# adaLN + S4D convolution + ReLU network on one NeuronCore: reordering the last kernel group, the transforms of block 0 and two DMA queues

## The chip, the cores and the metric

The kernel runs on one core of one Trainium2 chip. The metric is the device time of one execution in microseconds (us). The names of the engines in the profile are PE (TensorE matmul), PEld (TensorE weight load), DVE (VectorE), ACT (ScalarE), POOL (GpSimd) and SP (SyncE, which here only issues DMAs).

## The reference, cut to what matters

```python
def _A_ref(u, log_A_real, A_imag, C_real, C_imag, log_dt, D_skip):     # L = 2048, D = 576, N = 128
    dt = exp(log_dt); A = -exp(log_A_real) + 1j * A_imag; C = (C_real + 1j * C_imag) * dt[:, None]
    P = exp((A * dt[:, None])[:, :, None] * arange(L))
    K = 2.0 * einsum("dn,dnl->dl", C, P).real          # the generated convolution kernel
    Kf = rfft(K, 2 * L); Uf = rfft(u.T, 2 * L)
    return irfft(Uf * Kf)[:, :, :L].T + u * D_skip
def _B_ref(x, w1, w2):                                 # w1 576 x 4608, w2 4608 x 576
    return relu(x @ w1) @ w2
mod = (silu(c) @ w_mod)                                # 6 rows of 576: sa, ca, ga, sb, cb, gb
h = layernorm(x) * (1 + ca) + sa
x = x + ga * _A_ref(h, ...)
h = layernorm(x) * (1 + cb) + sb
x = x + gb * _B_ref(h, w1, w2)
```

## The kernel before

The sequence of 2048 is cut into 4 blocks of 512. Each block has a convolution part (`conv(s)`: transforms, spectra, products, inverse, second layernorm) and a part of the network (`ffn`, 36 column tiles of the hidden layer, each a `first` into `hps` and a `second` into `acc`). Matmuls are fp32 in two passes or split into a high and a low part in fp32r. Blocks 1 to 3 have their convolution woven into the network of the block before; block 0 has none before it, so everything up to its first `hps` matmul is a prologue.

The prologue generates the convolution kernel. 576 channels go in 6 groups of 96 (`KGen.first`, loop over `g`), each group in two halves `u` of 48. A group builds two factors on ACT, DVE and POOL: `W2` (32 powers) and `W1` (16 powers, by `doubling`: one, two, four, eight times two powers; the last doubling has the tiles `T0`, `T1` of 128 x 768 and its adds on POOL). The `products` of a half are 96 small matmuls, two passes each, from `W1` and `W2` into a PSUM tile `kps`. `rows(g)` copies `kps` into `ke` (ACT), and after every third group `store` writes `ke` to `kd` in DRAM; `load_kt` reads it back transposed as the tile `kt`, `skip` adds `D_skip` to its first row, and `mm_K` transforms it. `save(g)` stores `W1` to `W1d` for the later blocks.

`conv(0)` is a generator, run in `main`; what it yields as a word runs a piece of another: `"first"`, `"late"`, `"rows"` are the two halves of the last group's products and the end of `first` (`save(5)`, `rows(5)`, `store`), `"mod"` a step of `mod_late`, `"weights"`, `"high"`, `"low"` a step of `ffn` (loads of its first weights, their high parts, their low parts). `early` prepares `h`, the normalised and modulated input: its last step is `skip` on the first `kt` and, per row tile, a multiply by `ca` and an add of `sa`. `mm_U(p)` transforms half `p` of `h`, `mm_K(p)` half `p` of the kernel. `spec_U`, `spec_K` are the butterflies that make `U_0`, `U_1`, `K_0`, `K_1`; `product(p)` multiplies them to `Y`, `back` makes `V`, `inverse` transforms it back, and its result is added to `x` on DVE, between the steps of `product(1)`. `mod_late` makes `sb`, `cb` (in front of the network) and `gb` (behind it): loads of three pieces of `w_mod` (`wm_*`, 1.3 MB each), 50 small matmuls each (`mps_*`), a copy, and two transposes for `sb` and `cb` (`mpt_*`).

The order on an engine is that of a scheduler, except where an operation is recorded through `Kept` or `keep_in_program_order` (the profile then shows the helper's line, L47, L59, L62, L65, L68 or L71): those keep their written order against each other. Spectra tiles (`Z`, `W`, `U`, `K`, `Y`, `V`) share 6 buffers, and a tile starts only when the readers of its buffer, stores to DRAM included, are done. DMAs that an engine issues stand in its instruction queue and wait there in order.

Of the kernel before, what the change touches and what calls it, by code (L numbers as in the profile page):

```python
# [18 lines left out]
P = 128  # L19
# [30 lines left out]
class KGen:  # L50
# [274 lines left out]
    def first(self, setup, mod):  # L325
# [26 lines left out]
        def rows(g):  # L352
            qs = slice(24 * (g % 3), 24 * (g % 3) + 24)
            self.act(ke[:, :, qs], ps[g].rearrange("p q a -> p a q"), AF.Copy)
            if g % 3 == 2:
                self.store(0, g // 3, ke.rearrange("p a q -> p (a q)"), nc.sync)

# [39 lines left out]
        for g in range(NG):  # L397
# [26 lines left out]
            else:  # L424
                run(late, double[3])
            if g + 1 == NG:
                next(early)
            if g > 0:
                rows(g - 1)
            run(*double[4:])  # L430
            if g + 1 < NG:
                save(g)
# [141 lines left out]
class Body:  # L574
# [34 lines left out]
    def early(self, kg):  # L609
# [25 lines left out]
        for i in (0, 2, 1, 3):  # L635
            kept(nc.scalar.activation(
                h[:, i], x2[:, i], AF.Identity, scale=mv[:, i, 3:4], bias=mv[:, i, 4:5]
            ))
        yield
        self.kt0 = kg.kt0  # L640
        kept(self.skip(self.kt0, 0, nc.vector))
        for i in (0, 2, 1, 3):
            kept(nc.vector.tensor_tensor(h[:, i], h[:, i], self.m["ca"], op=ALU.mult))
            kept(nc.vector.tensor_tensor(h[:, i], h[:, i], self.m["sa"], op=ALU.add))
# [93 lines left out]
    def mod_late(self):  # L738


        nc, act, cb = self.nc, self.nc.scalar.activation, self.cb
        for j, nm in ((3, "sb"), (4, "cb"), (5, "gb")):
            self.mod_weights(self.wm[nm], slice(j * D, (j + 1) * D), nc.sync)
        for nm in ("sb", "cb", "gb"):
            yield
            w = self.wm[nm]
            ps = self.cps.tile([P, 512], F32, tag="cps", bufs=self.nps, name=f"mps_{nm}")
            self.mod_products(ps, cb, w, nc.tensor.matmul)
            row = self.cv.tile([P, 2 * P], F32, tag="row", bufs=1, name=f"row_{nm}")
            act(row[:, 0:P], ps[:, 0:P], AF.Copy)  # L750
            for o in (P, P + 64):
                act(row[0:32, o : o + 64], ps[0:32, P : P + 64], AF.Copy)
            if nm == "gb":
                yield
                self.mod_spread(row, self.md[nm], self.m[nm], Kept(self.tc, nc.gpsimd))
                return
            ps = self.cps.tile([P, 512], F32, tag="cps", bufs=self.nps, name=f"mpt_{nm}")
            nc.tensor.transpose(ps[:, 0:P], row[:, 0:P], self.ident)
            nc.tensor.transpose(ps[:, P : P + 32], row[0:32, P:], self.ident[:32, :32])
            act(  # L760
                self.m[nm], ps[:, 0 : 5 * 32].rearrange("p (j r) -> p j r", r=32)[:, :, 0],
                AF.Copy, bias=1.0 if nm == "cb" else 0.0,
            )

# [174 lines left out]
    def conv(self, s):  # L939
# [18 lines left out]
        def kernel_tile(p):  # L958
            t = self.cv.tile([P, 16, 72], F32, tag="kt", bufs=1, name="kt")
            self.load_kt(t, s, p, nc.gpsimd if s else nc.sync)  # L960
            return t

        kt = [kernel_tile(0) if s else self.kt0, None]
        yield -1 if s else "mod"
        if s:
# [15 lines left out]
        def spec_U(p, Z):  # L981
            U = self.spec(f"U_{s}_{p}")
            yield from self.butterfly(Z, U, -1)
            yield -1
            if s + 1 < NB or p == 1:
                self.save(self.Ud[s][p], U)
            Us.append(U if s == 0 or p == 0 else None)
# [87 lines left out]
        if s == 0:  # L1075
            yield from mm_K(0, ZK)
            yield from mm_U(0, ZU)
            Z1 = self.spec("Z")
            yield from mm_U(1, Z1)
            for hook in ("first", "late", "rows"):  # L1080
                yield hook
            kt[1] = kernel_tile(1)
            yield "weights"
            yield "mod"
            yield "mod"
            yield "mod"
            yield "high"
            yield from spec_U(0, ZU)
            yield from spec_U(1, Z1)
            yield from spec_K(0, ZK)  # L1090
            ZK = self.spec("Z")
            yield from mm_K(1, ZK)
            self.save(self.Rd[0][0], Ks[0], Kept(self.tc, nc.gpsimd))
        else:
            yield from both(self.norm1(x2, h), mm_K(0, ZK))
            kt[1] = kernel_tile(1)
            ZU = self.spec("Z")
            yield from both(spec_K(0, ZK), mm_U(0, ZU))
# [166 lines left out]
    def ffn(self, gens):  # L1265
# [166 lines left out]
        yield  # L1432
        lo1(0)
        lo2(0)
        lo1(1)
        yield
        load_r2(1)
# [200 lines left out]
```

## Time and profile before

| | |
|---|---|
| time, median of 3 runs | 1326.89 us |
| lowest, highest | 1318.24, 1328.18 us |
| the profiled execution's own time | 1322.81 us |
| its span (first to last instruction) | 1321.0 us |
| mean granted TensorE clock | 0.946 |
| PE busy over the span | 1210.7 us (92%) |
| DVE busy | 895.0 us (68%) |
| ACT busy, POOL busy | 494.8 us (37%), 160.3 us (12%) |
| PE busy from 345 us to the end | 961.21 of 976.00 us |
| DVE busy from 260 to 345 us | 83.71 of 85.00 us |

Times in the profile count from the span's first instruction. The first network matmul of block 0 (`hps`) starts at 220.30 us. A row of the timeline reads: start, duration, engine, line, operation, output<-inputs, shapes, count, and in brackets the idle time of the engine before it with what ended it.

### The profile page before, as it was taken

Reading aid. Unit: us, or ns where it says so; the run is one execution under the profiler, and the core shown is the slowest. Engines: PE = TensorE matmul, PEld = TensorE weight load, DVE = VectorE, ACT = ScalarE, POOL = GpSimd, SP = SyncE. Lnnn points to the kernel's source line nnn. Section 1 sums busy time; section 2 is a strip of 40 time slices with the busy share of each in tenths; the row PEclk is TensorE's granted clock in tenths of the full one; section 3 lists DMA queues with packets and bytes.
Section 4 is the critical chain, followed back from the end, with each engine's and each line's share of the span. In section 5 each row is a group of like instructions: output and inputs, shape, how many; then the busy total and the mean of one; then the engine's idle time right before and its main releaser. Section 6 shows DMA issues by size and latency. Waiting matters only on the chain.

```text
span 1321.0 us, 25994 instructions
## 1 busy us (share of the span) xinstructions
PE 1210.7 (92%) x10720; PEld 959.5 (73%) x10720; DVE 895.0 (68%) x1324; ACT 494.8 (37%) x863; POOL 160.3 (12%) x256
## 2 busy tenths in 40 slices
PE   4666686999999998999999999999999999999998
PEld 2444564677767776787777887887888888888886
DVE  7889988999976999589468994557996222111112
ACT  5787523222223422622243225433323452233231
POOL 1666411011000100110011000100000000000000
PEclk9556787999899999999999999999999999999999
DMA  8757982988778977799889985868996667666662
GB/s 274 269 200 289 322 304 85 349 308 322 286 256 303 345 241 262 261 406 336 279 276 336 360 323 156 294 198 294 343 382 198 172 179 227 202 194 197 195 178 71
DMA packets 118027, 345.85 MB, mean 262 GB/s; under 512 B 17772, under 2 KB 19604, under 8 KB 107156
## 3 DMA queue, kind: packets, MB, share of 16 engines
q1 hardware_dynamic: 101332, 228.14, 51.9%
q0 software_dynamic: 16064, 114.67, 23.0%
q8 instruction: 84, 1.38, 0.4%
q10 hardware_dynamic: 512, 1.38, 0.4%
q14 instruction: 35, 0.29, 0.1%
HBM read 262.73 MB, written 81.40 MB: 261 GB/s over the span
## 4 chain that ended last, share of the span: by engine, by line
PE 75%; DVE 14%; DMA 6%; issue 4%; ACT 1%; POOL 1%; SPq 0%; ACTq 0%; DVEq 0%; POOLq 0%
PE hps L1332 31%; PE acc L1358 30%; PE ps_f L852 5%; PE kps L519 3%; PE kps L71 2%; DMA L1d<-w 2%; PE ph L71 2%; PE ps_i L1059 2%; DVE T L484 1%; DVE W1r L486 1%; DMA x<-in_x_dram 1%; DVE T L62 1%; DMA Ua<-Ud 1%; DVE W L62 1%; DVE w L1302 1%
## 5 line engine op out<-in xcount | busy, mean ns | idle before, releaser
L1332 PE MATMUL hps<-xh,w 128*128 128x512 f32 x1152 | 394.2, 403 | 0.8 <-ACT xh L47 0.8
L1358 PE MATMUL acc<-w,hh 128*128 128x512 f32 x1136 | 362.1, 401 | 4.9 <-ACT hh L1337 3.4
L1338 DVE SCALAR_TENSOR_TENSOR hl<-hps,hh 128x512 fp32r<-128x512 f32 x144 | 99.2, 689 | 306.9 <-ACT hh L1337 306.2
L1332 PEld LDWEIGHTS hps<-xh,w 128*128 128x128 f32 x1152 | 217.8, 190 | 48.3 <-ACT xh L47 1.4
L1358 PEld LDWEIGHTS acc<-w,hh 128*128 128x128 f32 x1136 | 212.5, 188 | 51.3 <-ACT hh L1337 4.3
L1332 PE MATMUL hps<-xl,w 128*128 128x512 f32 x576 | 227.4, 396 | 0.0
L1358 PE MATMUL acc<-w,hl 128*128 128x512 f32 x568 | 221.0, 402 | 1.6 <-DVE hl L1338 1.6
L1337 ACT ACTIVATE hh<-hps 128x512 fp32r<-128x512 f32 x144 | 86.0, 597 | 324.7 <-PE hps L1332 317.5
L1307 ACT ACTIVATE w<-r 128x576 fp32r<-128x576 f32 x141 | 96.7, 686 | 229.0 <-PE acc L1358 221.4
L1332 PEld LDWEIGHTS hps<-xl,w 128*128 128x128 f32 x576 | 109.1, 189 | 22.9
L1358 PEld LDWEIGHTS acc<-w,hl 128*128 128x128 f32 x568 | 106.9, 190 | 25.3 <-DVE hl L1338 3.0
L1297 ACT ACTIVATE w<-r 128x640 fp32r<-128x640 f32 x140 | 102.6, 733 | 40.6 <-DMA L1d<-w 38.1
L1332 PE MATMUL hps<-xs,w 128*128 128x512 f32 x288 | 98.3, 411 | 0.0
L71 PE MATMUL kps<-W,W 128*32 128x16 f32 x2304 | 40.3, 211 | 44.9 <-POOL W L68 28.4
L1038 DVE TENSOR_TENSOR Y<-Y,T 128x1152 f32<-128x1152 f32 x60 | 79.4, 1351 | 0.0
L71 PEld LDWEIGHTS kps<-W,W 128*32 128x32 f32 x2304 | 35.5, 145 | 58.8 <-POOL W L68 31.0
L853 ACT ACTIVATE Z<-ps_f 128x288 f32<-128x288 f32 x120 | 48.9, 409 | 71.9 <-PE ps_f L852 70.1
L519 PEld LDWEIGHTS kps<-W1r,W2r 128*32 128x32 f32 x3456 | 45.1, 113 | 37.8 <-issue 23.1
L519 PE MATMUL kps<-W1r,W2r 128*32 128x48 f32 (+2 forms) x3456 | 52.5, 201 | 14.4 <-issue 8.8
L1332 PEld LDWEIGHTS hps<-xs,w 128*128 128x128 f32 x288 | 53.5, 189 | 11.2
L1358 PE MATMUL acc<-hh,w 128*128 128x512 f32 x142 | 56.7, 399 | 0.0
L1358 PE MATMUL acc<-hl,w 128*128 128x512 f32 x142 | 56.0, 394 | 0.0
(249 smaller groups left out, 1543.5 us busy)
## 6 DMA issues: line engine op xcount, KB each, us to landing
r<-in_w_dram SPq DMA_DIRECT2D x144, 320.0 KB, 5.9
r<-in_w_dram SPq DMA_DIRECT2D x144, 288.0 KB, 3.6
w<-L1d SPq DMA_DIRECT2D x108, 320.0 KB, 3.9
w<-L2d SPq DMA_DIRECT2D x108, 288.0 KB, 2.7
W2r<-W2d POOLq DMA_DIRECT2D x18, 1536.0 KB, 8.8
W2d<-W SPq DMA_DIRECT2D x12, 1536.0 KB, 8.5
Ua<-Ud POOLq DMA_DIRECT2D x15, 1152.0 KB, 9.4
W<-W1d POOLq DMA_DIRECT2D x18, 768.0 KB, 9.4
```

The costliest lines, as they stand in the source:

```text
L62: self.tc.keep_in_program_order(self.nc.vector.tensor_tensor(out, a, b, op=op))
L71: self.tc.keep_in_program_order(self.nc.tensor.matmul(*args, **kw))
L519: nc.tensor.matmul(ps[32 * dd : 32 * dd + 32, q, :], W2[:, r, ch], W1[:, r, ch], start=(r == 0), stop=(r == 1),)
L852: nc.tensor.matmul(o, fc[:, n2, c, :], src(n2), start=True, stop=True)
L853: ev = nc.scalar.activation(Z[:, n2, c], ps[:, :PC], AF.Copy)
L1038: v(y, y, T, op=op or ALU.add)
L1297: copy(g - 1)(w1[g][:, 0], r1[g], AF.Copy)
L1307: copy(g)(w[:, 0:D], r2[g], AF.Copy)
L1332: nc.tensor.matmul(ps, a, x, start=(i == 0), stop=(i == 13))
L1337: nc.scalar.activation(hh, ps, AF.Relu)
L1338: nc.vector.scalar_tensor_tensor(hl, ps, 0.0, hh, op0=ALU.max, op1=ALU.subtract)
L1358: nc.tensor.matmul(acc[i], a, x, start=(f == 0 and seen[i] == 1), stop=(f == NF - 1 and seen[i] == (3 if i < 4 else 2)),)
```

## The change

- `KGen.first`, last group: the step of `early` that shifts `h` is called behind the last doublings, not ahead of them; the `skip` of the first `kt` moves into the step before.
- `conv(0)`: the transforms and the last group's products alternate: `mm_K(0)`, first half of the products, `mm_U(0)`, second half and `rows`, `mm_U(1)`. The spectrum of `K_0` is made ahead of those of `U_0` and `U_1`.
- SP's queue: `W1d`, `kd` and `kt` of the last group stand ahead of the loads of `wm_sb`, `wm_cb`, `wm_gb`.
- `mod_late`: its matmuls stand behind `mm_K(1)`; the transposes of one piece stand behind the matmuls of the next.
- POOL's queue: the stores `Ud_0`, `Rd_0`, `Ud_1` of block 0's spectra stand in this order behind the `skip` of the second `kt`.
- `ffn`: its first loads (`"weights"`) come behind the spectra's stores; `"high"` and `"low"` come behind `inverse(0)`, and of the three low parts only the first stands there; the second and third come after the second layernorm.

```diff
@@ KGen.first
-                self.store(0, g // 3, ke.rearrange("p a q -> p (a q)"), nc.sync)
+                self.store(0, g // 3, ke.rearrange("p a q -> p (a q)"), Kept(self.tc, nc.sync))
...
                 run(late, double[3])
-            if g + 1 == NG:
-                next(early)
             if g > 0:
                 rows(g - 1)
             run(*double[4:])
+            if g + 1 == NG:
+                next(early)
@@ Body.early
-        yield
         self.kt0 = kg.kt0
         kept(self.skip(self.kt0, 0, nc.vector))
+        yield
         for i in (0, 2, 1, 3):
             kept(nc.vector.tensor_tensor(h[:, i], h[:, i], self.m["ca"], op=ALU.mult))
@@ Body.mod_late
-            self.mod_weights(self.wm[nm], slice(j * D, (j + 1) * D), nc.sync)
+            self.mod_weights(self.wm[nm], slice(j * D, (j + 1) * D), Kept(self.tc, nc.sync))
+        yield
+        rows = {}
         for nm in ("sb", "cb", "gb"):
-            yield
-            w = self.wm[nm]
             ps = self.cps.tile([P, 512], F32, tag="cps", bufs=self.nps, name=f"mps_{nm}")
...
-            row = self.cv.tile([P, 2 * P], F32, tag="row", bufs=1, name=f"row_{nm}")
+            row = rows[nm] = self.cv.tile([P, 2 * P], F32, tag="row", bufs=2, name=f"row_{nm}")
...
+            nm = {"cb": "sb", "gb": "cb"}.get(nm)
+            if nm:
+                row = rows[nm]
+                ps = self.cps.tile([P, 512], F32, tag="cps", bufs=self.nps, name=f"mpt_{nm}")
+                nc.tensor.transpose(ps[:, 0:P], row[:, 0:P], self.ident)
+                nc.tensor.transpose(ps[:, P : P + 32], row[0:32, P:], self.ident[:32, :32])
...
+            yield
+        self.mod_spread(rows["gb"], self.md["gb"], self.m["gb"], Kept(self.tc, nc.gpsimd))
@@ Body.conv
-            self.load_kt(t, s, p, nc.gpsimd if s else nc.sync)
+            self.load_kt(t, s, p, nc.gpsimd if s else Kept(self.tc, nc.sync))
...
-            if s + 1 < NB or p == 1:
+            if s and (s + 1 < NB or p == 1):
                 self.save(self.Ud[s][p], U)
...
             yield from mm_K(0, ZK)
+            yield "first"
             yield from mm_U(0, ZU)
+            yield "late"
+            yield "rows"
             Z1 = self.spec("Z")
             yield from mm_U(1, Z1)
-            for hook in ("first", "late", "rows"):
-                yield hook
             kt[1] = kernel_tile(1)
-            yield "weights"
             yield "mod"
-            yield "mod"
-            yield "mod"
-            yield "high"
+            yield from spec_K(0, ZK)
             yield from spec_U(0, ZU)
             yield from spec_U(1, Z1)
-            yield from spec_K(0, ZK)
             ZK = self.spec("Z")
             yield from mm_K(1, ZK)
-            self.save(self.Rd[0][0], Ks[0], Kept(self.tc, nc.gpsimd))
+            for dst, t in (
+                (self.Ud[0][0], Us[0]), (self.Rd[0][0], Ks[0]), (self.Ud[0][1], Us[1])
+            ):
+                self.save(dst, t, Kept(self.tc, nc.gpsimd))
+            for _ in range(3):
+                yield "mod"
+            yield "weights"
...
         if s == 0:
-            yield "low"
             yield from spec_K(1, ZK)
...
             yield from inv
+            yield "high"
+            yield "low"
             yield "mod"
@@ Body.ffn
         lo1(0)
+        yield
+        lo1(1)
         lo2(0)
-        lo1(1)
-        yield
```

**PE**, from the end of the fifth group's products to the inverse transform. `kps_1942` is the fifth group, `kps_2248` the sixth (its two rows are the two halves), `ps_f<-kt_1943` is `mm_K(0)`, `ps_f<-h_2099` is `mm_U`, `ps_f<-kt` is `mm_K(1)` (16 rows, of which the first stands here). Before:

```order
L71 MATMUL kps_1942<-W_4_1712,W_9_1706 32x16 x96
L852 MATMUL ps_f<-kt_1943,fcK 128x288 x8
L852 MATMUL ps_f<-h_2099,fcU 128x288 x16
L71 MATMUL kps_2248<-W_5_2048,W_10_2041 32x16 x96
L71 MATMUL kps_2248<-W_5_2048,W_11_2042 32x16 x96
L733 MATMUL mps_sb<-wm_sb,cb 32x128 x20
L758 MATMUL mpt_sb<-ident,row_sb 128x128
L733 MATMUL mps_cb<-wm_cb,cb 32x128 x19
L758 MATMUL mpt_cb<-ident,row_cb 128x128
L733 MATMUL mps_gb<-wm_gb,cb 32x128 x19
L891 MATMUL ps_f<-kt,fcK 128x288
L1059 MATMUL ps_i<-V_0_2753,gc 128x288 x6
```

The same place with the change:

```order
L71 MATMUL kps_1942<-W_4_1712,W_9_1706 32x16 x96
L854 MATMUL ps_f<-kt_1943,fcK 128x288 x8
L71 MATMUL kps_2248<-W_5_2048,W_10_2041 32x16 x96
L854 MATMUL ps_f<-h_2099,fcU 128x288 x8
L71 MATMUL kps_2248<-W_5_2048,W_11_2042 32x16 x96
L893 MATMUL ps_f<-kt,fcK 128x288
L733 MATMUL mps_sb<-wm_sb,cb 32x128 x20
L733 MATMUL mps_cb<-wm_cb,cb 32x128 x20
L757 MATMUL mpt_sb<-ident,row_sb 128x128
L733 MATMUL mps_gb<-wm_gb,cb 32x128 x20
L757 MATMUL mpt_cb<-ident,row_cb 128x128
L1062 MATMUL ps_i<-V_0_2746,gc 128x288 x6
```

The sixth group's halves now stand on either side of the first `mm_U` (a second row of 8 `ps_f<-h_2099` follows the second half), and the modulation's matmuls have moved from ahead of `mm_K(1)` to between it and the inverse transform `ps_i`.

**SP**, the DMA queue behind the stores of the last `W2` factors. Before:

```order
L723 DMA wm_sb<-in_w_mod_dram 128x4x576
L723 DMA wm_gb<-in_w_mod_dram 128x4x576
L723 DMA wm_cb<-in_w_mod_dram 128x4x576
L360 DMA W1d_87<-W_5_2048 256x1x768
L360 DMA W1d_88<-W_5_2048 256x1x768
L452 DMA kd_1_58<-ke_1607 64x1152 x2
L1255 DMA kt<-kd_1_58 128x16x72
L47 DMA r_2560<-in_w_dram 128x640
```

With the change:

```order
L360 DMA W1d_87<-W_5_2048 256x1x768
L360 DMA W1d_88<-W_5_2048 256x1x768
L47 DMA kd_1_58<-ke_1607 64x1152 x2
L47 DMA kt<-kd_1_58 128x16x72
L47 DMA wm_sb<-in_w_mod_dram 128x4x576
L47 DMA wm_cb<-in_w_mod_dram 128x4x576
L47 DMA wm_gb<-in_w_mod_dram 128x4x576
L47 DMA r_2731<-in_w_dram 128x640
```

The store of the kernel's rows and the load of the second `kt` now stand ahead of the three `wm` loads, and these wait in the queue until `kt` has been issued. (Each `wm` load has a second row of 64 x 576, left out here.) Farther down this queue, the stores of the network's low parts `L1d_1` and `L2d_0` and the loads behind them wait for the second and third low parts, which are now made after the second layernorm.

More of the change, by code (lines that the diff above doesn't have):

```diff
@@ L742, in mod_late @@
         for j, nm in ((3, "sb"), (4, "cb"), (5, "gb")):
-            self.mod_weights(self.wm[nm], slice(j * D, (j + 1) * D), nc.sync)
+            self.mod_weights(self.wm[nm], slice(j * D, (j + 1) * D), Kept(self.tc, nc.sync))
+        yield
+        rows = {}
         for nm in ("sb", "cb", "gb"):
-            yield
-            w = self.wm[nm]
             ps = self.cps.tile([P, 512], F32, tag="cps", bufs=self.nps, name=f"mps_{nm}")
-            self.mod_products(ps, cb, w, nc.tensor.matmul)
-            row = self.cv.tile([P, 2 * P], F32, tag="row", bufs=1, name=f"row_{nm}")
+            self.mod_products(ps, cb, self.wm[nm], nc.tensor.matmul)
+            row = rows[nm] = self.cv.tile([P, 2 * P], F32, tag="row", bufs=2, name=f"row_{nm}")
             act(row[:, 0:P], ps[:, 0:P], AF.Copy)
@@ L752, in mod_late @@
                 act(row[0:32, o : o + 64], ps[0:32, P : P + 64], AF.Copy)
-            if nm == "gb":
-                yield
[L755 to L763, printed above, removed]
+            nm = {"cb": "sb", "gb": "cb"}.get(nm)
[4 more added lines that the diff above has]
+                nc.tensor.transpose(ps[:, P : P + 32], row[0:32, P:], self.ident[:32, :32])
+                act(
+                    self.m[nm], ps[:, 0 : 5 * 32].rearrange("p (j r) -> p j r", r=32)[:, :, 0],
+                    AF.Copy, bias=1.0 if nm == "cb" else 0.0,
+                )
+            yield
+        self.mod_spread(rows["gb"], self.md["gb"], self.m["gb"], Kept(self.tc, nc.gpsimd))
+        yield
     def pool(self, ctx, name, **kw):
@@ L959, in kernel_tile @@
             t = self.cv.tile([P, 16, 72], F32, tag="kt", bufs=1, name="kt")
-            self.load_kt(t, s, p, nc.gpsimd if s else nc.sync)
+            self.load_kt(t, s, p, nc.gpsimd if s else Kept(self.tc, nc.sync))
             return t
         kt = [kernel_tile(0) if s else self.kt0, None]
-        yield -1 if s else "mod"
+        if s:
+            yield -1
         if s:
@@ L1433, in ffn @@
         lo1(0)
+        yield
+        lo1(1)
         lo2(0)
-        lo1(1)
-        yield
         load_r2(1)
```

## The prediction

> **What bounds the kernel now.** I read the busy times by stretch first, because the page's totals (PE 92%) hide that only one stretch can be changed.
>
> ```profile
> core 0: us, PE busy (x) PEld busy (x) DVE busy (x) ACT busy (x) POOL busy (x), PEclk, DMA share, GB/s
> ...
> 183.20:191.50 8.30, 8.30 (x35) 6.49 (x35) 2.37 (x6) 4.37 (x10) 0.00 (x0) 1.00 1.02 398
> ...
> 260.00:345.00 85.00, 76.57 (x1390) 59.80 (x1391) 83.71 (x89) 20.21 (x37) 9.52 (x18) 0.96 0.85 310
> 345.00:1321.00 976.00, 961.21 (x6021) 771.49 (x6019) 583.33 (x818) 333.83 (x599) 51.80 (x90) 1.00 0.76 258
> ```
>
> From 345 us on PE is busy 98.5% and the change touches nothing there. From 220 to 345 the network of block 0 is bound by DVE (98% busy from 260). What comes earlier at 220 us is therefore handed through to the end, unless the start of the network pays for it. Before 220 us DVE is the bound, with one hole: 183.2 to 191.5, where it works 2.37 of 8.30 us. What made the hole is in the chain that ended last and in DVE's timeline:
>
> ```profile
> 173.11 2.55 DMA kd<-ke
> 175.71 5.39 DMA kt<-kd
> 181.27 1.31 POOL kt L47
> 182.58 8.80 DMA Rd<-K
> ```
>
> ```profile
> 149.95 3.54 DVE L62 TENSOR_TENSOR T<-W,Zp 128x768 f32<-128x768 f32 x4
> 153.97 4.23 DVE L47 TENSOR_TENSOR W<-Z 128x576 f32<-128x576 f32 x4 [0.48 <-ACT Z L853]
> ...
> 183.16 0.81 DVE L47 TENSOR_TENSOR w<-r,w 128x640 fp32r<-128x640 f32 x1
> 184.38 1.56 DVE L47 TENSOR_TENSOR w<-r,w 128x64 fp32r<-128x64 f32 x3 [0.40 <-ACT w L47]
> 191.47 2.90 DVE L47 TENSOR_TENSOR K<-Z 128x576 f32<-128x576 f32 x6 [5.53 <-DMA Rd<-K]
> ...
> 200.45 0.45 DVE L47 TENSOR_TENSOR x<-ps_i,x 128x288 f32<-128x288 f32 x1
> ...
> 202.20 1.36 DVE L47 TENSOR_TENSOR Y<-Y,T 128x1152 f32<-128x1152 f32 x1
> ...
> 226.85 0.69 DVE L1338 SCALAR_TENSOR_TENSOR hl<-hps,hh 128x512 fp32r<-128x512 f32 x1 [1.48 <-ACT hh L1337]
> ```
>
> `K_1` could not begin until its input (the transform `mm_K(1)`) and its buffer (the store `Rd`) were there, and both hang on the same trip: last products, `ke`, `kd`, `kt`, `skip`. So the end of the sixth group's products, E below, sets the prologue. PE's timeline around it:
>
> ```profile
> 140.75 0.66 PE L71 MATMUL kps<-W,W 128*32 128x16 f32 x31 [1.78 <-issue]
> 144.39 7.09 PE L852 MATMUL ps_f<-kt,fcK 128*128 128x288 f32 x16 [2.98 <-issue]
> 151.32 7.92 PE L852 MATMUL ps_f<-h,fcU 128*128 128x288 f32 x32
> 159.18 1.82 PE L71 MATMUL kps<-W,W 128*32 128x16 f32 x174
> 166.68 1.95 PE L71 MATMUL kps<-W,W 128*32 128x16 f32 x128 [5.68 <-issue]
> 170.68 1.31 PE L71 MATMUL kps<-W,W 128*32 128x16 f32 x81 [2.05 <-issue]
> ...
> 171.83 3.31 PE L733 MATMUL mps_sb<-wm_sb,cb 128*32 128x128 f32 x48
> ...
> 179.69 2.22 PE L733 MATMUL mps_gb<-wm_gb,cb 128*32 128x128 f32 x48
> 182.68 0.75 PE L891 MATMUL ps_f<-kt,fcK 128*128 128x288 f32 x2 [0.77 <-POOL kt L47]
> ...
> 190.54 3.07 PE L1059 MATMUL ps_i<-V,gc 128*128 128x288 f32 x12
> ...
> 197.81 0.65 PE L1059 MATMUL ps_i<-V,gcn 128*128 128x288 f32 x2
> 207.17 6.43 PE L1059 MATMUL ps_i<-V,gc 128*128 128x288 f32 x16 [8.71 <-DVE V L47]
> ```
>
> Three things are to be seen. E was 170.68 + 1.31 = 171.99. The products stop twice for "issue", 5.68 and 2.05 us, with exactly 128 matmuls between the stops. And the modulation's matmuls (171.83 to 181.91, 10.1 us) cost nothing, since PE would have waited for `kt` until 182.68 anyway.
>
> **The change part by part.** The sum is made against the profiled execution, 1322.81 us (span 1321.0), 4.1 under the median of 1326.89.
>
> *Doublings first.* The last four doublings leave DVE 6.2 us earlier, at 143.74 + the moved `skip`, so POOL's adds and the products' input too. DVE's work is only reordered: it runs without a hole from 153.97 to 183.16 and still does, less the 0.48. Gain on DVE by itself: none.
>
> *E.* PE can begin `mm_K(0)` at 141.4, as its `skip` is no longer behind the doublings: 7.1 us, to 148.5. First half of the products 2.9, `mm_U(0)` 4.0, second half 2.9: E = 158.3 without a stop. The stops go with the count of matmuls (128 to a batch), not with their place. From 140.75 on, the stream holds 31 + 16 + 192 + 16 + 192, so a batch ends inside the first half, at the start of the second and two thirds into it. One stop should vanish behind `mm_U(0)`. The other two cost 2.05 to 5.68 each: E between 162.4 and 169.7. With fewer loads in flight I am nearer the low row: **E = 163.5**, bounds 158.3 and 169.7, 8.5 us earlier than now.
>
> *The trip* E to `mm_K(1)` stays 182.68 - 171.99 = 10.7 us, and `mm_K(1)` 190.54 - 182.68 = 7.9. Its result is then there near 183. The spectra's stores lose their early start and go out behind the `skip`, at E + 10.7.
>
> ```profile
> Ud<-U POOLq DMA_DIRECT2D x2, 1152.0 KB, 8.1
> ```
>
> That of `U_0`, whose buffer `K_1` now takes, lands 8.1 us later, also near 183; `Y_1` takes the buffer of `K_0` 2.9 us after. The next readers of these stores are the later blocks, far off. DVE reaches `K_1` at 182.8, so all three cost nothing, or a microsecond if E is late. So the hole closes; if nothing else were late, `Y_1` would end 12.1 us later, at 194.9, where it now ends at 203.56: the largest gain there can be, 8.7 us.
>
> *What is late next: the modulation's matmuls.* They have lost their cover and stand between `mm_K(1)` and `ps_i`, whose results DVE adds between the steps of `Y_1`. Three times 2.22 us and four transposes, between 6.7 and the 10.1 of today; I take 8.3. They end at E + 10.7 + 7.9 + 8.3 = E + 26.9 if PE is not slowed and the weights are there. `ps_i` takes 198.46 - 190.54 = 7.9, and the last add and what follows it in `Y_1` 203.56 - 200.45 = 3.1. `Y_1` then ends at E + 38.
>
> Both conditions are doubtful. After 8.71 us of idle PE ran 16 matmuls of `ps_i` in 6.43 us, 0.40 each, against 0.25 before; in the new order PE is idle some 6.7 us (10.7 less 4.0 of `mm_U(1)`) ahead of `mm_K(1)`. The price is 0 to 2.4 us. And the weights:
>
> ```profile
> q1 hardware_dynamic: 1300, 2.87, 104.4%
> ```
>
> ```profile
> q0 software_dynamic: 241, 1.98, 79.3%
> q1 hardware_dynamic: 127, 0.34, 14.2%
> ```
>
> The first is SP's queue from 152 to 160 us, weights alone: 0.36 MB per us. The others are 166 to 172 us, with POOL storing spectra: POOL's queue 0.33 MB per us, SP's 0.06. With the change 4.0 MB of weights are issued behind `kt` (E + 4) and move from about E + 8; the three stores, 3.5 MB, start to move near E + 13. The weights have 1.8 MB by then, 0.6 in the 10.7 us of the stores, and the rest by E + 27.5; without the stores by E + 19. `mps_gb` alone needs the last of them, so the delay is 0 to 3 us. I take 1.5 for clock and weights together: **`Y_1` ends at E + 39.7 = 203.2, 0.4 us earlier than now.**
>
> Two rules of the Trainium skill bear on these two prices. DMA: Bandwidth & Descriptors (Queues, rings and completion order) says that each DMA engine goes round between the queues it has work for, a packet at a time; by this the large packets of the stores take most of an engine while they last, as in the rows above, and the weights' delay would be the 3 us; with equal shares it would be none. TensorE: Matmul & The Clock Gate (Part 1) says the clock halves after an idle window of about 3.4 us; by that the 6.7 us of idle are enough and the full 2.4 us are due; by the row alone, idle of 8.71 us, they may not be. With both rules in full `mps_gb` ends at E + 30 and the sum below at 1326.5; with neither it is 1323.3.
>
> *Low parts.* Of the 2.4 us of `w<-r` in the old hole, 0.8 now stand on DVE's path ahead of `V_1`, the rest behind the second layernorm, where DVE waited 1.5 us for `hh`: together +1.1.
>
> *The network's start.*
>
> ```profile
> 188.47 0.53 SPq L1449 DMA_DIRECT2D L1d<-w  x1
> ```
>
> ```profile
> 231.12 0.73 ACT L1297 ACTIVATE w<-r 128x640 fp32r<-128x640 f32 x1
> ...
> 235.77 0.60 ACT L1337 ACTIVATE hh<-hps 128x512 fp32r<-128x512 f32 x1 [2.49 <-DVE W1r L490]
> 245.84 0.74 ACT L1297 ACTIVATE w<-r 128x640 fp32r<-128x640 f32 x1 [9.47 <-DMA L1d<-w]
> ```
>
> ```profile
> 239.03 0.84 PE L1358 MATMUL acc<-w,hh 128*128 128x512 f32 x3
> ```
>
> ```profile
> q0 software_dynamic: 704, 4.60, 76.0%
> q1 hardware_dynamic: 641, 1.40, 24.2%
> ```
>
> S is the first `hps` matmul, 220.30 today. Until now the stores of the first low parts went out by 189 us, long before S. With the change `L1d_1`, `L2d_0` and the two loads ahead of them in SP's queue, 1.2 MB, can go only some 6 us after S, when POOL fetches the later blocks' factors: in the 15 us from 230 to 245 (the two rows) its queue moved 4.60 MB, SP's 1.40, or 0.09 MB per us. 1.2 MB at that rate are 13 us. The high part at 231.12, S + 10.8, needs the buffer that `L1d_1` frees; it and the next would stand in ACT's queue until S + 15 to S + 22, and `hh` behind them (235.77, S + 15.5) is what PE's next `acc` matmuls wait for. PE has a few idle moments later to win some back: 0 to 5 us. I take 1.5, nearer to nothing: ACT stood idle for 9.47 us just behind, at 245.84, so most of such a wait only moves.
>
> Sum: -0.4 + 1.1 + 1.5 = **+2.2, so 1325 us**. A run's own scatter (1318.24 to 1328.18 before) is as large; 1% of the median, 13 us, is about what a measurement of this kernel can tell from no change.
>
> **The rivals.**
>
> *The hole closes and little takes its place.* The stops hide behind the alternation, E is 159 to 161, the clock stays up and the weights are there: `Y_1` ends at E + 38, 197 to 199, 5.5 us earlier; less 1.1 for the low parts: 1318. For it: the stops come with the count of matmuls, and the transforms give the fetch time. Against it: the three `mps` were free and now are not.
>
> *The network's start pays.* All as forecast, but ACT's queue does stand for `L1d_1` and `L2d_0`: 5 us in place of 1.5, 1329; it decides as soon as `hh` of the third tile comes later than 18.7 us after S, where PE's `acc` takes it (239.03). For it: the two DMA rows. Against: the 9.47 us.
>
> *The products are not earlier.* Each batch waits 4 us or more, and the transforms between run at 0.44 a matmul, as the first 16 do today, in place of 0.25: E is 169, `Y_1` ends at 208.7, with the rest 1330 to 1333. For it: the 5.68 stop. Against: it came while the queues were full of the weights, which now stand behind.
>
> **How the numbers follow.** Forecast 0.45 (its own range 1320 to 1330), the closed hole 0.25 (1314 to 1320), the network's start 0.20 (1327 to 1334), no earlier products 0.10 (1328 to 1337). All but 2 in 10 lie between 1315 and 1335; the run's scatter is within that, as the cases lean to both sides. The largest gain of 8.7 us less 1.1 would be 1315, still inside 1%; 1% and more either way needs a case that I have not seen, or an unlucky pair of runs: faster 0.06, same 0.89, slower 0.05.
>
> **What would show it.** E (end of the last `kps` of the prologue) near 163.5, after two stops for "issue", the first of them in the first half. DVE without a hole at `K_1`, near 183, and a new one at the first `x<-ps_i`, of some 5 us, ended by PE. `mps_gb` waiting for a DMA, or ending near E + 28. The last `Y` before `V_1` ending at 203. `hps` starting within 3 us of 220.3. ACT standing before the high part of the fifth tile for `L1d`. From 345 us on nothing but a shift. I am wrong if DVE's hole at `x<-ps_i` is under 2 us (then the gain is 5 or more), if `hps` starts later than 225, or if the time changes at a place behind 345 us.

## The result, and the profile after

The changed kernel is slower: median 1332.7 us (1325.19 to 1341.4, 20 runs) against 1324.86 (1312.3 to 1330.81, 20 runs) for the kernel before, ratio 1.0067 with a 95% interval of 1.0049 to 1.0085, some 8 us. The profiled execution took 1333.06 us (span 1330.9), 9.9 us of span more than that of before. Of these, 2.7 us stand ahead of the first `hps` (its start is called S: 223.03, was 220.30) and 7.2 behind it (S to the end of the span: 1107.9, was 1100.7).

PE's timeline of the changed kernel at the place of the change (start, duration, ..., idle before with its cause):

```profile
148.13 2.07 PE L71 MATMUL kps<-W,W 128*32 128x16 f32 x190 [0.72 <-POOL W L68]
...
156.66 1.40 PE L71 MATMUL kps<-W,W 128*32 128x16 f32 x125
159.17 0.84 PE L71 MATMUL kps<-W,W 128*32 128x16 f32 x67 [1.12 <-issue]
...
176.34 1.33 PE L893 MATMUL ps_f<-kt,fcK 128*128 128x288 f32 x2 [12.25 <-POOL kt L47]
...
186.94 2.22 PE L733 MATMUL mps_sb<-wm_sb,cb 128*32 128x128 f32 x50
...
191.68 2.22 PE L733 MATMUL mps_gb<-wm_gb,cb 128*32 128x128 f32 x50
...
194.26 3.18 PE L1062 MATMUL ps_i<-V,gc 128*128 128x288 f32 x12
```

The sixth group ends at 159.17 + 0.84 = 160.0 (E), 12 us earlier than before, after one short stop in place of two. But PE then stands 12.25 us for the skip of `kt`, and `mm_K(1)` takes 10.6 us (176.34 to 186.94) in place of 7.9. The chain that ended last and POOL's timeline say why:

```profile
163.65 4.33 DMA kt<-kd
168.14 8.15 POOL kt L47
```

```profile
168.14 8.14 POOL L47 TENSOR_TENSOR kt<-kt,m_gb 1x288 f32<-1x288 f32 x1 [17.11 <-DMA kt<-kd]
176.23 0.56 POOL L47 DMA_DIRECT2D Ud<-U  x1
```

`kt` was there at 168.1, 13 us earlier than before, but the addition of 288 numbers on one partition took 8.14 us; before the change it took 1.35. DVE's timeline:

```profile
186.52 2.90 DVE L47 TENSOR_TENSOR K<-Z 128x576 f32<-128x576 f32 x6 [3.56 <-ACT Z L896]
...
196.51 0.46 DVE L47 TENSOR_TENSOR x<-ps_i,x 128x288 f32<-128x288 f32 x1 [5.83 <-PE ps_i L1062]
...
204.09 1.36 DVE L47 TENSOR_TENSOR Y<-Y,T 128x1152 f32<-128x1152 f32 x1
```

The hole ahead of `K_1` shrank, a new one stands at the first `x<-ps_i`, and the last `Y` ends at 205.45 (203.56 before). Behind the first `hps`, SP's queue, ACT's timeline and PE's waits (the last from 212 to 270 us; us in total, times, longest):

```profile
229.97 0.79 SPq L1456 DMA_DIRECT2D L1d<-w  x1
230.81 0.54 SPq L1456 DMA_DIRECT2D L2d<-w  x1
```

```profile
242.98 0.74 ACT L1304 ACTIVATE w<-r 128x640 fp32r<-128x640 f32 x1 [9.03 <-DMA L1d<-w]
246.48 0.68 ACT L1314 ACTIVATE w<-r 128x576 fp32r<-128x576 f32 x1 [2.76 <-DMA L2d<-w]
247.06 0.58 ACT L1344 ACTIVATE hh<-hps 128x512 fp32r<-128x512 f32 x1
```

```profile
PE acc L1365 <- ACT hh L1344: 5.8, 1, 5.8
```

`L1d_1` and `L2d_0` leave the queue 7 us behind S. ACT stands for them, and the third `hh` behind them comes 24.0 us after S, where it came 15.5 after S before; PE stands 5.8 us for it. Behind this stop PE also runs slower. Busy times from 240 to 260 us (the granted clock of PE is third from the right), before and then changed:

```profile
240.00:260.00 20.00, 17.29 (x386) 12.61 (x385) 18.50 (x20) 5.34 (x10) 2.12 (x4) 1.00 0.87 321
```

```profile
240.00:260.00 20.00, 14.22 (x140) 10.51 (x138) 14.42 (x16) 5.66 (x9) 1.07 (x2) 0.83 0.89 350
```

### The profile page after: what moved, and what is told of

Same layout as the page of the kernel before. It is cut to its first block, busy times and chain, and to the rows that moved or that the text cites. A ratio compares the mean times of both kernels' runs of the same rounds, so it can differ in the third digit from the quotient of the medians.

```text
span 1330.9 us, 25993 instructions
## 1 busy us (share of the span) xinstructions
PE 1213.8 (91%) x10720; PEld 958.0 (72%) x10720; DVE 896.4 (67%) x1324; ACT 495.0 (37%) x863; POOL 167.7 (13%) x256
## 4 chain that ended last, share of the span: by engine, by line
PE 70%; DVE 10%; DMA 6%; issue 2%; ACT 1%; POOL 1%; SPq 0%; DVEq 0%; ACTq 0%; POOLq 0%
PE hps L1339 29%; PE acc L1365 29%; PE ps_f L854 4%; DMA L1d<-w 3%; PE kps L519 2%; PE ps_i L1062 2%; DMA L2d<-w 1%; DVE Y L1041 1%; DMA Zr<-Zd 1%; DMA Ua<-Ud 1%; DVE T L1039 1%; DVE T L484 1%; DVE W1r L486 1%; DMA r<-in_w_dram 1%; POOL kt L47 1%
## 5 line engine op out<-in xcount | busy, mean ns | idle before, releaser
L1365 PEld LDWEIGHTS acc<-w,hl 128*128 128x128 f32 x568 | 106.2, 188 | 24.8 <-DVE hl L1345 2.7
```

The source lines that it names most:

```text
L1365: nc.tensor.matmul(acc[i], a, x, start=(f == 0 and seen[i] == 1), stop=(f == NF - 1 and seen[i] == (3 if i < 4 else 2)),)
```

## The experiments

All ratios are to the kernel before, run on the same chip, with 95% intervals. E is the end of the sixth group's products and S the start of the first `hps`. The times in the middle are from the one profiled execution of each kernel, and not every one is typical: those of e5_alt, e8_mods and e9_mods_skip were the slowest of their kernels' 12 runs (4.6 to 6.4 us above the median), that of e11_mods_low the fastest of 12 (3.4 us below). S to the end also varies between kernels by some us for reasons that the runs do not show, so the column of the third `hh` is the sharper one.

| kernel | E | `mm_K(1)` | last `Y` ends | S | third `hh` - S | S to end | median | ratio |
|---|---|---|---|---|---|---|---|---|
| before | 172.0 | 182.7-190.7 | 203.6 | 220.3 | 15.5 | 1100.7 | 1322.1 to 1324.9, by chip | 1 |
| changed | 160.0 | 176.3-187.0 | 205.5 | 223.0 | 24.0 | 1107.9 | 1332.7 | 1.0067 [1.0049, 1.0085] |
| e12_split_only | 172.5 | 186.8-194.8 | 206.4 | 223.7 | 23.9 | 1105.9 | 1330.9 | 1.0060 [1.0040, 1.0080] |
| e1_low | 159.5 | 175.5-185.9 | 208.5 | 225.4 | 15.2 | 1103.2 | 1328.6 | 1.0034 [1.0013, 1.0054] |
| e4_gap | 161.6 | 171.0-181.6 | 208.7 | 226.5 | 24.0 | 1109.8 | 1338.4 (1 run) | |
| e2_skip | 160.2 | 169.7-180.2 | 204.7 | 222.4 | 24.0 | 1106.2 | 1331.3 | 1.0064 [1.0041, 1.0086] |
| e3_both | 158.3 | 167.3-175.3 | 208.5 | 225.2 | 15.4 | 1100.7 | 1327.8 | 1.0038 [1.0019, 1.0056] |
| e5_alt | 164.2 | 184.3-193.8 | 205.4 | 222.2 | 15.2 | 1108.2 | 1325.8 | 1.0025 [1.0000, 1.0049] |
| e6_alt_skip | 163.3 | 182.6-193.1 | 204.8 | 221.8 | 15.2 | 1102.4 | 1325.1 | 1.0005 [0.9980, 1.0030] |
| e7_wmfirst | 162.8 | 177.5-187.1 | 209.7 | 226.4 | 15.2 | 1104.7 | 1332.6 | 1.0065 [1.0041, 1.0089] |
| e8_mods | 161.6 | 177.6-188.0 | 199.6 | 216.9 | 24.8 | 1111.7 | 1325.3 | 1.0005 [0.9982, 1.0028] |
| e9_mods_skip | 162.2 | 171.4-181.1 | 196.8 | 213.8 | 24.9 | 1114.2 | 1325.6 | 1.0007 [0.9986, 1.0028] |
| e10_mods_skip_low | 159.6 | 168.8-178.5 | 194.2 | 212.9 | 15.4 | 1104.0 | 1316.8 | 0.9935 [0.9909, 0.9961] |
| e11_mods_low | 158.9 | 174.9-185.6 | 197.2 | 215.9 | 15.5 | 1101.4 | 1322.7 | 0.9996 [0.9978, 1.0013] |

**The network's start: e1_low (in the changed kernel) and e12_split_only (in the kernel before).**

```diff
# e1_low, against the changed kernel: ahead of spec_K(1), not behind inverse(0)
+            yield "high"
+            yield "low"
             yield from spec_K(1, ZK)
# and in ffn
-        lo1(0); yield; lo1(1); lo2(0)
+        lo1(0); lo2(0); lo1(1); yield
# e12_split_only, against the kernel before, in ffn
-        lo1(0); lo2(0); lo1(1); yield
+        lo1(0); yield; lo1(1); lo2(0)
```

> The changed kernel, but all three low parts are made together again ahead of the spectrum of K_1 (and the high parts ahead of them), so that L1d_1, L2d_0 and the loads behind them leave SP's queue before the network starts. Theory N (the network's start pays: in the changed kernel the third hh comes 24.0 us after the first hps, 15.5 before the change, as ACT's queue stands for L2d_0, which landed 15.6 us after its issue): the third hh is back at 15 to 17 us after the first hps, the way from the first hps to the end of the span goes from 1107.9 back to 1101, and the time is 6 us lower than that of the changed kernel, near 1326.5. The low parts themselves (2.4 us of DVE) fall into the hole of 3.6 us ahead of K_1 and cost nothing; the first hps stays near 222. Rival (the loss behind the first hps is from something else, such as POOL's later loads or the phase in which kernel generation meets the network): the third hh stays beyond 20 us or the way to the end stays above 1106, and the time stays at 1331 to 1334.

> The kernel before with one part of the change alone: the second and third low parts come behind the second layernorm, the first stays ahead of K_1. Theory N: the prologue stays as it is (first hps 220 to 221), L1d_1 and L2d_0 leave SP's queue some 6 us behind the first hps, the third hh comes 22 to 25 us after it (15.5 before), and the time is 4 to 7 us above the kernel before: ratio 1.003 to 1.005. Rival G (the network evens out such waits behind 260, where DVE is the bound): the third hh is late, but the way from the first hps to the end stays at 1097 to 1100 and the time within 2 us of the kernel before.

Theory N (the split low parts cost time at the network's start) holds in both directions. Together, the low parts bring the third `hh` back to 15.2 us behind S; split, in a kernel that is otherwise that of before, it comes 23.9 us behind S, and this one edit makes the kernel 0.60% slower, as much as the whole change within the intervals and somewhat more than expected. ACT's timeline of e12_split_only reads as that of the changed kernel:

```profile
243.45 0.74 ACT L1297 ACTIVATE w<-r 128x640 fp32r<-128x640 f32 x1 [8.85 <-DMA L1d<-w]
246.95 0.68 ACT L1307 ACTIVATE w<-r 128x576 fp32r<-128x576 f32 x1 [2.77 <-DMA L2d<-w]
247.54 0.58 ACT L1337 ACTIVATE hh<-hps 128x512 fp32r<-128x512 f32 x1
```

Its S is also 3.4 us late. The half clock at which PE ran from 165 to 185 us in this execution began ahead of the low parts, which DVE made only at 183 us in the kernel before; whether it comes with the edit, one execution can't show (a row of the windows, granted clock third from the right):

```profile
175.00:180.00 5.00, 4.63 (x52) 2.82 (x49) 4.93 (x5) 0.65 (x4) 0.00 (x0) 0.50 0.74 196
```

The way from S to the 36th `hh`, the last of block 0, shows what the low parts' place is worth beside that. Against the kernel before it is 5.1 us longer in e12_split_only and 6.3 in the changed kernel. In pairs of kernels that differ in the low parts it falls from 6.3 to -0.4 (changed, e1_low), from 5.5 to -2.2 (e2_skip, e3_both) and from 11.4 to 0.4 (e9_mods_skip, e10_mods_skip_low). In e5 to e7, whose low parts are together and whose third `hh` is in time, it is still 1.9 to 5.6 us longer; why stays open.

In e1_low one point of the expectation failed: the low parts were not free. DVE waited 12.04 us for ACT's high parts, which stood behind the copies of the modulation's rows, and S came 2.4 us later; the gain was 4 us and not 6. DVE's row:

```profile
194.20 2.30 DVE L47 TENSOR_TENSOR w<-r,w 128x640 fp32r<-128x640 f32 x4 [12.04 <-ACT w L47]
```

**POOL's skip: e4_gap, e2_skip, e3_both.** Against the changed kernel:

```diff
# e4_gap, spec_U(1): two one-column copies on DVE
+                tiny(gap[:, 0:1], W[:, 3, 1, 287:288])      # behind butterfly1
+                tiny(gap[:, 1:2], U[:, 2, 1, 287:288])      # behind the first pair of butterfly2
# e2_skip
-                self.skip(kt[p], p, Kept(self.tc, nc.gpsimd))              # in mm_K
+                self.skip(kt[1], 1, Kept(self.tc, nc.vector))              # between butterfly1 and butterfly2 of U_1
# e3_both: the edits of e1_low and e2_skip
```

> The changed kernel with two one-column copies on DVE, each of the element that the operation just ahead of it wrote: one behind the first half of U_1's butterflies, one behind its first pair of the second half. Each must wait until that write is done, so DVE's chain of overlapping operations has a gap near 169.0 and near 170.5, where it had its first one at 175.64 in the changed kernel. Theory P in its narrow form (POOL gets at the memory only when DVE's overlapping chain breaks): POOL's skip takes 1 to 3 us in place of 8.14, and mm_K(1) begins at 169.5 to 171.5. Rival (POOL's skip is slow by itself, or its input is late): still 7 to 8 us, mm_K(1) at 175 to 177.

> The changed kernel, but the skip of the second kt is done by DVE between the two halves of U_1's butterflies instead of by POOL. Theory P (POOL's skip, 8.14 us in the changed kernel and 1.35 before, was ready at 168.1 and stood for DVE's tensor operations): the DVE skip takes 0.4 to 1.4 us as soon as kt has landed, mm_K(1) begins near 169.5 in place of 176.3, the last Y ahead of V_1 ends 5 to 7 us earlier than 205.45 (4 if the weights are then late because the stores of the spectra now go out at 166), and the time falls by as much, to 1326 to 1329. Rival (kt was not there before 175.6, or POOL's own work was long): DVE stands for kt until about 175, mm_K(1) begins at 175 or later and the time stays at 1331 to 1334.

> Both edits at once: the low parts together ahead of K_1, and the second skip on DVE. If theories N and P hold, their gains add: 6 + 5, to 1320 to 1323, faster than the kernel before by 2 to 5 us. The low parts are then no longer in a hole (K_1 does not wait once mm_K(1) starts at 169.5), but DVE would stand for ps_i anyway, so they still cost nothing. If only one holds: 1326 to 1329. If the prologue's gain is lost in the network (DVE bound from 260 on, loads no earlier): 1325 to 1327.

POOL's and DVE's timelines of e4_gap:

```profile
170.13 0.85 POOL L47 TENSOR_TENSOR kt<-kt,m_gb 1x288 f32<-1x288 f32 x1 [17.78 <-DMA kt<-kd]
```

```profile
168.25 2.09 DVE L47 TENSOR_TENSOR W<-Z 128x576 f32<-128x576 f32 x3
170.37 0.15 DVE L47 COPY gap<-W 128x1 f32<-128x1 f32 x1
170.44 1.83 DVE L47 TENSOR_TENSOR U<-W 128x576 f32<-128x576 f32 x2
```

With a break in DVE's chain the skip takes 0.85 us: theory P (POOL's skip stands for DVE) in its narrow form. (Its one time, 1338.4, is no verdict; `mps_gb` began only at 190.7 and the last `Y` ended at 208.7, so at the end nothing was gained.) On DVE itself (e2_skip) it takes 0.44 and `mm_K(1)` starts 6.7 us earlier. But the time did not follow, since the next wait stood right behind it. PE's timeline of e2_skip:

```profile
180.16 2.22 PE L733 MATMUL mps_sb<-wm_sb,cb 128*32 128x128 f32 x50
185.64 3.86 PE L733 MATMUL mps_cb<-wm_cb,cb 128*32 128x128 f32 x50 [3.26 <-DMA wm_cb<-in_w_mod_dram]
...
190.08 3.08 PE L733 MATMUL mps_gb<-wm_gb,cb 128*32 128x128 f32 x50
```

The weights, now behind `kt` in SP's queue, come at 185 and later, `ps_i` starts at 193.5 (194.3 in the changed kernel), and the ratio stays at 1.0064. So the expected 5 to 7 us fell to less than one: the skip was one of two waits in a row. e3_both adds only e1_low's gain.

**The weights and the matmuls back where they were: e5_alt, e6_alt_skip, e7_wmfirst.**

```diff
# e5_alt, against the kernel before: of the change only
#   KGen.first and Body.early (doublings ahead of h's shift), and in conv
+            yield from mm_K(0, ZK); yield "first"; yield from mm_U(0, ZU); yield "late"; yield "rows"
+            yield from mm_U(1, Z1)
# e6_alt_skip: e5_alt, and behind the first two multiplications of product(0)
+            self.skip(kt[1], 1, Kept(self.tc, nc.vector))
# e7_wmfirst, against the changed kernel: DVE's skip at that place, e1_low's edit, and
+        yield -1 if s else "mod"        # the loads of wm_* ahead of mm_K(0), unkept, as before
```

> The kernel before with two parts of the change alone: the last doublings ahead of h's shift, and the sixth group's products alternating with the transforms on PE. The modulation's loads and matmuls, the queues, the order of the spectra and the low parts are as before. Theory M (the alternation gains, and what lost it is the move of the modulation's weights and matmuls from behind the products to behind mm_K(1)): E at 160 to 168 in place of 172.0; the three mps fill the wait for kt and skip; mm_K(1) starts at 174 to 177 (POOL's skip may stand until DVE's first dependent operation near 175.6) at full clock, 7.9 us long, with no matmul between it and ps_i; K_1 at 184 to 186 in place of 191.5, the last Y ahead of V_1 ends at 197 to 199 in place of 203.6, first hps near 214.5, and the way from there to the end as before (within 2.5 us): 1317 to 1321, ratio 0.994 to 0.998. Rival Q (with the weights in flight during the products PE stops for instructions as long as before): E 169 or later, and the time is that of before within 2 us. Rival G (an earlier start is given back in the network, where DVE is the bound and loads are no earlier): first hps 4 us or more earlier, but the way to the end longer by as much.

> The same as the run with the alternation alone, but the second skip is done by DVE behind the first two multiplications of Y_0 (near 174.3). Theory M with P: the skip takes 0.4 to 0.5 us, mm_K(1) starts at 174.8 or when the mps are done (E + 10), whichever is later; the last Y ahead of V_1 ends at 196 to 198, time 1316 to 1320, the lowest of all kernels here, 0 to 2 us under the alternation alone. Rival: kt comes later than 174.3 (E later than 166), DVE stands for it, and the time is that of the alternation alone or higher.

> The changed kernel with three edits: the second skip on DVE behind the first two multiplications of Y_0, the three low parts ahead of K_1, and the wm loads ahead of W1d, kd and kt in SP's queue as before the change; the modulation's matmuls stay behind mm_K(1). It differs from the kernel with the alternation and DVE's skip mainly in that place of the matmuls, and from the kernel with both edits in the order of the loads. Theory M: no mps waits for a DMA any more, but they stand uncovered: mm_K(1) starts near 174.8 after 7 to 11 us of idle PE, so at half clock for 5 us, and takes 10.6; mps until 192.6, ps_i until 200.6, the last Y ahead of V_1 ends at 203 to 205, no better than the kernel before; time 1323 to 1327, 5 to 8 us above the kernel with the alternation and DVE's skip. Rival W (only the weights' lateness mattered, not the place of the matmuls): the last Y ends at 197 to 200 and the time is within 3 us of that kernel.

Theory M (the alternation gains, and the moved matmuls lost it) failed here in a way that I had not listed. E came at 163 to 164, but `mm_U(1)` now stands behind the products, and DVE, which in these kernels makes `U_1` ahead of `K_0`, waited for it. PE's and DVE's timelines of e6_alt_skip:

```profile
162.13 1.15 PE L71 MATMUL kps<-W,W 128*32 128x16 f32 x67 [5.02 <-issue]
```

```profile
167.89 1.43 DVE L47 TENSOR_TENSOR W<-Z 128x576 f32<-128x576 f32 x2 [7.38 <-ACT Z L853]
```

What the products gained on PE, the spectra lost on DVE. By this trace the order of the spectra is a needed part of the change; no run tests it alone. The first row shows what putting the weights behind `kt` is worth: with them in flight the stop for "issue" is 4.59 to 5.34 us (e5 to e7), without them 1.12 to 1.64 (changed, e1 to e4, e8 to e11). In the traces of before, changed, e3_both and e6_alt_skip a packet of 16 KB on a queue of kind "instruction" lands 1.2 to 1.5 us ahead of the end of such a stop; by this timing, PE waits there for its instructions. e7_wmfirst fitted neither theory: no `mps` waited for a load, as M said, but `ps_i` was done at 202.4 (M: 200.6), DVE again stood 9.85 us for the high parts, and the last `Y` ended at 209.7, later than in both. Its time lies 0.6% above that of e6_alt_skip, as M said, but as the 9.85 us are in it, this does not separate M from W.

**The matmuls out of the way: e8_mods, e9_mods_skip, e10_mods_skip_low, e11_mods_low.** Against the changed kernel:

```diff
# e8_mods, conv(0)
-            for _ in range(3):
-                yield "mod"
             yield "weights"
...
             yield from inv
+            for _ in range(3):
+                yield "mod"
...
         yield from back(1, Y)
+        if s == 0:
+            yield "high"
+            yield "low"
# and a buffer of its own for wm_gb
# e9_mods_skip: with e2_skip's edit; e10_mods_skip_low: also lo1(0); lo2(0); lo1(1) together
# e11_mods_low: e10_mods_skip_low with the skip on POOL
```

> The changed kernel, with the modulation's three groups of matmuls moved from between mm_K(1) and ps_i of V_0 to behind that ps_i, into the 7.4 us in which PE otherwise waits for V_1. (So that this can be done, gb's weights have a buffer of their own, and the high and low parts stand behind V_1.) POOL still does the second skip, so mm_K(1) comes as late as in the changed kernel (176.3 to 187.0). Theory M2 (the uncovered matmuls, and the weights they wait for, are what K_1's gain was lost to): K_1 near 186.5, no hole of DVE at the first x<-ps_i, the last Y ahead of V_1 ends at 198 to 200 in place of 205.45, first hps near 216, time 5 to 7 us under the changed kernel, 1326 to 1328. Rival (the matmuls only move the wait: ps_i of V_1 then comes late): the last Y ends earlier but ps_i of V_1 starts at 209 or later as before, first hps at 221 or later, time 1331 to 1334.

> The same with the second skip on DVE, between the halves of U_1's butterflies. With the matmuls in their old place DVE's skip brought mm_K(1) 6.7 us forward and the last Y only 0.75, as the weights came at 185 to 190. Theory P + M2: with the matmuls out of the way the skip is worth what K_1 gains: mm_K(1) 169 to 180, K_1 at 183 without a wait of DVE, the last Y ends at 195 to 197, first hps near 213; 2 to 4 us under the run with the moved matmuls alone, 1322 to 1325. Rival (skip is worth nothing anywhere): the last Y as in the run with the moved matmuls, 198 or later.

> The same again, with all three low parts together behind V_1. Theory N: 1.6 us more of DVE ahead of the first hps (near 214.5), and L1d_1 and L2d_0 leave SP's queue before it, so the third hh is back at 15 to 17 us after the first hps (24 in the changed kernel) and the way to the end at 1098 to 1101: 3 to 5 us under the run without it, 1317 to 1321, below the kernel before (1323 to 1325). Rival G (what the prologue gains is given back in the network, where DVE is the bound from 260 on): the way to the end grows as the start comes forward, and the time is within 2 us of the kernel before.

> The fastest kernel so far (matmuls of the modulation behind ps_i of V_0, DVE's skip, all low parts together), with the second skip given back to POOL. Theory P: POOL's skip again takes 7 to 8 us, K_1 waits 3 us, the last Y ahead of V_1 ends 4 to 5 us later (199.6 in the run with the moved matmuls and POOL's skip, 194.2 in the fastest), and since the network's start no longer hides anything this arrives at the end: 3 to 5 us slower than with DVE's skip, 1320 to 1322, ratio 0.996 to 0.999. Rival (what POOL's wait costs is given back in the network, as the runs without the low parts suggest, 1325.3 with POOL's and 1325.6 with DVE's skip): 1316 to 1318.

PE's timeline of e10_mods_skip_low, then ACT's:

```profile
168.81 0.72 PE L896 MATMUL ps_f<-kt,fcK 128*128 128x288 f32 x2 [3.41 <-DVE kt L47]
...
180.27 3.15 PE L1069 MATMUL ps_i<-V,gc 128*128 128x288 f32 x12 [1.77 <-issue]
...
188.20 2.22 PE L733 MATMUL mps_sb<-wm_sb,cb 128*32 128x128 f32 x50
...
192.94 2.22 PE L733 MATMUL mps_gb<-wm_gb,cb 128*32 128x128 f32 x50
...
197.79 5.40 PE L1069 MATMUL ps_i<-V,gc 128*128 128x288 f32 x15 [2.20 <-DVE V L47]
```

```profile
223.65 0.73 ACT L1312 ACTIVATE w<-r 128x640 fp32r<-128x640 f32 x1
...
228.30 0.60 ACT L1352 ACTIVATE hh<-hps 128x512 fp32r<-128x512 f32 x1 [2.49 <-DVE W1r L490]
```

Theory M2 (the uncovered matmuls ate the gain of `K_1`) holds for the prologue: moved into a stretch in which PE waited for `V_1` anyway, the matmuls cost next to nothing, their weights have time to come, the last `Y` ends at 199.6 and, with DVE's skip, at 196.8. S came 6 and 9 us earlier than in the changed kernel, and the time fell by 0.6% in both. Whether e9's further 3.1 us at S reached the end can't be told: they are 0.23%, and the intervals of both kernels are 0.2% to either side. With the low parts together, e10_mods_skip_low is 0.65% faster than the kernel before (0.42% by the medians on that chip, 1316.8 against 1322.4) and the fastest here. The third `hh` is 15.4 us behind S again, and 0.7% lie between it and e9_mods_skip. Giving the skip back to POOL (e11_mods_low) costs 3 us at S, and the ratio goes from 0.9935 to 0.9996, more than expected; the two profiled executions have nearly equal spans (1316.9 and 1317.3), but e11's was the fastest of its 12, so where the rest lies stays open.

## Why the prediction was wrong, point by point

The profiles differ by 9.9 us of span, where the sum had 2.2. Ahead of S it had 0.4 us and the runs showed 2.7; behind S it had 1.8 and the runs showed 7.2. So the step that failed most is the network's start, and the next is the trip from E to `mm_K(1)`.

- **E: right in kind, better than forecast.** 160.0 against 163.5. I counted two stops; the one in the first half did not come, and the one in the second half was 1.12 us, with the weights behind `kt`.
- **The trip from E to `mm_K(1)`: failed.** I carried 10.7 us over from the trace of before; it was 16.3, though `kt` itself came 8.1 us after E (9.3 before). The skip took 8.14 us, a cost that I had read from a single row (1.35) without asking what DVE did beside it; the sum had no term for it.
- **The clock: right place, somewhat more than its price.** `mm_K(1)` took 2.7 us longer, after 12.25 us of idle PE; the forecast had 0 to 2.4 us after 6.7, and 1.5 in the sum for clock and weights together.
- **The modulation's matmuls: right.** 7.3 us uncovered (forecast 8.3), a new hole of 5.83 us at the first `x<-ps_i` (forecast some 5). The weights were not late, but only because `mm_K(1)` was; once it came early (e2_skip) they were, by 3.26 us at `mps_cb` (forecast 0 to 3).
- **The last `Y`**: 205.45, forecast 203.2; E's 3.5 us were gained and the trip's 5.6 lost. That it came so near is in part luck, as the two errors have opposite signs. **Low parts**: from the last `Y` to S 17.6 us, 0.8 more than before, as forecast.
- **The network's start: the step that failed.** The term was mis-sized: 1.5 us in the sum, 5 in a rival of 0.20; in the profiles 7.2, and 0.60% alone in e12_split_only. The mechanism, the place (ACT ahead of the fifth tile, for `L1d`) and the condition were right: the rival decided as soon as the third `hh` came later than 18.7 us after S, and it came at 24.0. My own estimate of S + 15 to S + 22 already reached beyond it. I discounted it with ACT's idle of 9.47 us just behind; but that idle is ACT's, and what counts is PE. Its reserve was 2.7 us: before, the third `hh` was done at S + 16.1 and PE took it at S + 18.7. The `hh` came 8.6 us later, and less the reserve that is about the 5.8 us for which PE stood. The slower clock behind the stop, for which the sum had nothing, came on top.
- **The sum itself** has two small slips: 38 + 1.5 is 39.5 and not 39.7, and with the rates given the weights are there by E + 28 and not E + 27.5.

The range held the time (1332.7 in 1315 to 1335), but the forecast of 1325 saw next to no change, and a clear loss of some 8 us came. Of the rivals the network's start was nearest (1329), with S some 2.3 us later than in it (220.3 - 0.4 + 0.8 = 220.7, measured 223.0).

## What to carry to other kernels

A step that is split and half put off also puts off every DMA that waits for it, and what stands behind those in an in-order queue; price that by the engine that waits at the end of the queue, not by idle time of one in the middle. When work loses its cover, look for the next stretch in which its engine waits anyway: the same three groups of matmuls cost 7 us in one place and next to nothing 9 us later (186.9 in the changed kernel, 195.7 in e8_mods). A small operation on POOL beside a busy DVE has no fixed duration: here the same addition took 0.85 to 8.14 us.

## What the runs showed of the hardware

**POOL's small addition stood until DVE's chain broke, with two exceptions.** The profiles show DVE's additions and multiplications of two operands overlapping by 0.08 us from one to the next, except where one needs the result of the one just ahead (a gap of 0.03 us). In the five profiles in which POOL's skip became ready within such a chain of `U`, `K` and `Y` operations (changed, e1, e5, e8, e11) it took 6.71 to 8.14 us and ended 0.6 us behind the first gap, at `Y<-Y,T`, whose own duration rose from 1.36 to 1.83. In e4_gap, where the copies put a gap in earlier, it also ended 0.6 us behind that gap. The place in the changed kernel:

```profile
174.29 1.35 DVE L47 TENSOR_TENSOR T<-K,U 128x1152 f32<-128x1152 f32 x1
175.67 1.83 DVE L47 TENSOR_TENSOR Y<-Y,T 128x1152 f32<-128x1152 f32 x1
```

The Trainium skill, page "SBUF — State Buffer", section "Who interferes with whom", says that a DVE instruction with two SBUF inputs contends with a GpSimd instruction that reads SBUF, and calls the port pair that they share an exclusive lock. The traces agree on the contention, but POOL waited here over eight to ten further instructions of DVE, and not only for the one that was running. In two executions (before, e12_split_only) POOL got in between two overlapping `V<-Y` after 0.7 us or less; why there is not shown.

**PE's clock.** `mm_K(1)` took 8.0 us after 3.19 us of idle PE (e3_both) and 9.5 to 10.7 after 3.41 to 12.25 us (the other kernels with the alternation). This agrees, with only one kernel below it, with the idle window of about 3.4 us of "TensorE: Matmul & The Clock Gate" (Part 1) in the Trainium skill.
